# Attention and channel mix on one core: float32 product with v in the first eight heads, first head turned by TensorE

## The chip, the cores and the metric

The kernel runs on one core of one Trainium2 chip. The time is device time in microseconds (us) for one execution. A core has five engines that run side by side, each through its own list of instructions in order: TensorE (PE; its weight loads are shown apart, as PEld), VectorE (DVE), ScalarE (ACT), GpSimd (POOL) and SyncE (SP), which here issues all DMAs. [...]

## The reference

Batch 8, 8 heads, 1152 tokens, head size 64. Pairs of queries are averaged, so that each head has 576 queries and 1152 keys:

```
q_pool = q.reshape(B, H, S // 2, 2, D).mean(axis=3)
scores = (1 / sqrt(D)) * q_pool @ k^T
attn   = exp(scores - max);  attn = attn / (sum(attn) + 1e-9)
x      = attn @ v              # heads side by side: [8, 576, 512]
xk, xr = mu * x + (1 - mu) * (x shifted by one token)     # with mu_k, mu_r
kk     = relu(xk @ w_k);  vv = (kk * kk) @ w_v
out    = sigmoid(xr @ w_r) * vv
```

All is float32, with w_k 512 x 1024, w_v 1024 x 512 and w_r 512 x 512.

## The kernel before

TensorE takes float16 operands here, so every float32 operand is split into a high part (its float16 value) and a low part (the rest), and a product is made of two or three matmuls.

**Heads.** The 64 heads (n = 0 to 63, batch n // 8) come one after the other. `prep` (L421) loads a head's keys and values (`kr`, `vr`), splits the keys into high and low halves side by side in `kn` (L433 ScalarE, L438 VectorE for the first head, else GpSimd), turns `kn` by a transposing DMA into `ks1` (L441: upper 64 partitions the high, lower 64 the low halves) and copies the upper halves into `ks2` by another DMA (L444). It splits the scaled values into `vt` (high L449 ScalarE, low L452 VectorE) and makes `vb` (L455 GpSimd), a scaled float16 copy. `queries` (L387) does the like for a pair of heads: adds pairs of queries, splits, and turns by DMA (L416).

**Blocks.** A head has six blocks of 96 queries (`block`, L462). Scores of the nine key tiles go to PSUM (L482); VectorE takes the maximum over the tiles (L489); TensorE turns it (L492), VectorE ends the maximum (L495), TensorE spreads it (L497), ScalarE writes it as a row of the queries' low part (L500); the second scores (L506) add the low parts and take the maximum away. ScalarE's exponential (L512), shifted by 18, writes float32 weights to `pf`. The product then uses the upper 16 bits of each weight as a float16 number, read in place, and the lower 16 bits as an integer, which GpSimd scales to float16 in `pl` (L515; for the first 64 rows of a head into `pf` itself).

**Windows.** The product with v (`window`, L525) goes by five windows of up to 128 queries; the first holds 64 rows, its upper half and lower-bit half side by side ("side"). For each of nine key tiles there are two matmuls with the weights' upper bits (L541 with 65 columns, one of them the sum of the weights; L543 with 64), and one with the lower bits (L548). After the last window the side window's two halves are joined (L565, L567), and the rows are divided by their sums (L569 to L572). Every second head the result is turned into `xt`: in batch 0 by float32 transposes on TensorE (L597, L600), later by DMA.

**Weights.** w_k, w_r and w_v come in 20 tiles of 128 x 512 float32 (`weights`, L608) while the heads of batch 0 run. Each is split: absolute value on ScalarE (L630), the lowest bits from the top bytes of the low words on ScalarE (L633), two integer operations on VectorE (L635, L637), high part on ScalarE (L645), low part on GpSimd (L646).

**Feed-forward.** When all heads of a batch are done, tiles of 256 tokens go through `ff` (L693, matmuls at L709) between the heads of later batches.

**Order of work.** All of this is first noted as operations with an engine, a duration, the buffers read and written, and a due time (`op`, class `Issue`). A planner plays these durations through on a model of the engines, tries several orders, keeps the best by its own reckoning and writes the instructions of every engine in that order. The durations in the calls of `op` thus set the order, and changing one may change the order anywhere. To the planner DMA is one engine; `tail` is the time from its end to the landing.

The lines that the rest speaks of are in these functions.

Of the kernel before, what the change touches and what calls it, by code (L numbers as in the profile page):

```python
# [4 lines left out]

# [6 lines left out]
F32 = mybir.dt.float32  # L12
# [18 lines left out]
SQ = 0.25  # L31

# [3 lines left out]
LO, VLO = 2.0 ** -28, 2.0 ** -12  # L36
GUARD = 1e-9 * math.exp(SHIFT) * 2.0 ** -40
# [222 lines left out]
def kernel(  # L260
# [58 lines left out]
    nc.gpsimd.tensor_copy(identb, ident)  # L319
    negi = const.tile([P, P], F16, name="negi")  # L320
# [8 lines left out]
    qn = bufs("qn", 1, [P, 2, NQ, P], F16)  # L329
# [33 lines left out]
    def mus(n, m):  # L363
        t_ = const.tile([P, NG], F32, name=f"mu_{n}")
        o = const.tile([P, NG], F32, name=f"omu_{n}")
        mu[n] = (t_, o)
        op("DMA", 0.46, lambda: nc.sync.dma_start(t_, m.rearrange("(c p) -> p c", p=P)), w=[("mu", n)], key=60.0)
        sk = SK if n == "k" else 1.0
        op("DVE", 0.1, lambda: nc.vector.tensor_scalar(o, t_, -sk, sk, op0=ALU.mult, op1=ALU.add),
           r=[("mu", n)], w=[("omu", n)], key=62.0)  # L370
# [4 lines left out]
    nc.gpsimd.memset(qn[0][:, 1, :, D:P], 0.0)  # L375
    for t_ in ks2:
        nc.vector.memset(t_[D:P], 0.0)
        nc.vector.memset(t_[QN:QN + 1], SM)
    for t_ in vt:
        nc.vector.memset(t_[:, :, 2 * D:2 * D + 2], 1.0)  # L380
# [6 lines left out]
    def queries(n, key):  # L387

        b, h = divmod(n, H)
        i = n // 2 % 2  # L390
        qv = q[b, h:h + 2].rearrange("h (t f) d -> (h t) (f d)", f=2).rearrange("(j p) x -> p j x", p=P)
        JS = ((0, 5), (5, NQ))
        for j0, j1 in JS:
            js = slice(j0, j1)
            op("DMA", 0.36, lambda js=js: nc.sync.dma_start(qr[0][:, js], qv[:, js]), w=[("qr", j0)],
               key=key - 2 * NB * PER, tail=3.0)
            op("DVE", (j1 - j0) * D / 960 + 0.069, lambda js=js: nc.vector.tensor_tensor(
                qs[0][:, js], qr[0][:, js, 0:D], qr[0][:, js, D:2 * D], op=ALU.add),
               r=[("qr", j0)], w=[("qs", j0)], key=key, port=True)
            op("ACT", (j1 - j0) * P / 1200 + 0.093, lambda js=js, j1=j1, j0=j0: nc.scalar.activation(  # L400
                qn[0][:, 0, js].rearrange("p j (r d) -> p j r d", r=2),
                qs[0][:, js].unsqueeze(2).broadcast_to([P, j1 - j0, 2, D]), AF.Copy, scale=SQ),
               r=[("qs", j0)], w=[("qn", j0)], key=key + 1)
            op("DVE", (j1 - j0) * D / 960 + 0.069, lambda js=js: nc.vector.scalar_tensor_tensor(
                qn[0][:, 1, js, 0:D], qs[0][:, js], SQ, qn[0][:, 0, js, 0:D], op0=ALU.mult, op1=ALU.subtract),
               r=[("qs", j0), ("qn", j0)], w=[("qnl", j0)], key=key + 2, port=True)
            if n and j0 == 0:
                continue

            g0 = 0 if n else j0  # L410
            gs = slice(g0, j1)
            blocks = [(hh, jj, g) for g, g1 in JS for hh in (0, 1) for jj in range(NB)
                      if g0 <= g < j1 and hh * TQ + jj * QN < g1 * P and hh * TQ + (jj + 1) * QN > g * P]
            js_ = [g for g, _ in JS if g0 <= g < j1]
            for r_, m, t_ in ((0, "qn", "qT"), (1, "qnl", "qTl")):
                op("DMA", 1.25, lambda gs=gs, r_=r_: nc.sync.dma_start_transpose(  # L416
                    qT[i][:, r_, gs], qn[0][:, r_, gs].rearrange("p j x -> p (j x)")),
                   r=[(m, g) for g in js_] + ([("qn", g) for g in js_] if r_ else []),
                   w=[(t_, i) + b_ for b_ in blocks], key=key + 2, tail=2.0)

    def prep(n, key):  # L421
# [3 lines left out]
        def dma(o, src, buf):  # L425
# [3 lines left out]
        dma(vr[i], v[b, h].rearrange("(p c) d -> p c d", c=NC), ("vr", i))  # L429
        for c0, c1 in ((0, 5), (5, NC)):  # L430
# [10 lines left out]
        op("DMA", 1.3, lambda: nc.sync.dma_start_transpose(ks1[i], kn[i].rearrange("p c x -> p (c x)")),  # L441
           r=[(m, i, c0) for m in ("kn", "knl") for c0 in (0, 5)], w=[("ks1", i, 0), ("ks1", i, 5)],
           key=key + 1, tail=2.0)
        op("DMA", 0.47, lambda: nc.sync.dma_start(ks2[i][0:D], ks1[i][0:D]),  # L444
           r=[("ks1", i, 0), ("ks1", i, 5)], w=[("ks2", i)], key=key + 1, tail=2.5)
# [16 lines left out]
    def block(n, j, i, t):  # L462
# [49 lines left out]
        op("ACT", NC * QN / 1200 + 0.051, lambda: nc.scalar.activation(  # L512
            pf[:, :, HALF + rows.start:HALF + rows.stop], grid(0, NC), AF.Exp, bias=SHIFT, scale=0.125 / (2.0 * SQ)), r=[("s", z)], w=[("pf", j)], key=t + O_EXP)
# [11 lines left out]
    def window(n, w, t):  # L525
# [12 lines left out]

        def hi(c0, c1):
# [11 lines left out]
        for c0 in (0, 3, 6):  # L551
            op("PE", 3 * 0.0595, lambda c0=c0: hi(c0, c0 + 3),
               r=vk + [("pf", j) for j in js] + ([("pside",)] if side else []) + ([("a",)] if c0 or w else []),
               w=[("a",)], key=t)
        for c0, c1 in () if side else ((0, 5), (5, NC)):
# [9 lines left out]
        op("ACT", 0.34, lambda: nc.scalar.activation(cross[up], a_b[0:HALF, 0:VN], AF.Copy, scale=VLO),  # L565
           r=[("a",)], w=[("cross",)], key=t + O_EVAC)
        op("DVE", 0.36, lambda: nc.vector.tensor_tensor(a_b[up, 0:VN], a_b[up, 0:VN], cross[up], op=ALU.add),  # L567
           r=[("cross",), ("a",)], w=[("a",)], key=t + O_EVAC)
        op("DVE", 0.075, lambda: nc.vector.tensor_scalar(dz, u[:, :, D], GUARD, None, op0=ALU.add),  # L569
# [7 lines left out]
        if n >= H:  # L577
# [5 lines left out]
            for kx, x, to in (("xbh", xbh, xth), ("xbl", xbl, xtl)):  # L583
                op("DMA", 0.8, lambda x=x, to=to: nc.sync.dma_start_transpose(to.rearrange("p (k x) -> p k x", k=NW), x),
                   r=[(kx,)], w=[(kx, "t"), *old[1]], key=t + O_TURN, tail=2.0)
# [22 lines left out]
    def weights(n, w, kc, key, step):  # L608
        cols = w.shape[1]
        wv = w.bitcast(I32).rearrange("(c p) (f t) -> c p f t", p=P, t=2)  # L610
        for c in range(kc):
            for f in range(0, cols, 512):
# [9 lines left out]
                op("DMA", 0.36, lambda s3=s3, src=wv[c, :, f:f + 512]: nc.sync.dma_start(s3, src),  # L622
                   r=[("ks1", 1, 0), ("ks2", 0), ("vr", 1)] if iss.nw <= 2 else [], w=[ks, kl], key=key, tail=4.5)
# [8 lines left out]
                if True:  # L632
                    op("ACT", 0.57, lambda wl=wl, tops=tops: nc.scalar.activation(wl, tops, AF.Copy, bias=-0.49, scale=2.0 ** -5),  # L633
                       r=[ks, kl], w=[kl], key=key)
                    v_(0.6, lambda ui=ui, wl=wl: nc.vector.scalar_tensor_tensor(  # L635
                        ui, ui, 3, wl, op0=ALU.logical_shift_left, op1=ALU.bitwise_or), [kl, kf], [kf])
# [56 lines left out]
    def ff(t0, t1, key, tail):  # L693
# [49 lines left out]
        for s0 in range(0, n, P):  # L743
# [103 lines left out]
```

## Time and profile before

| | |
|---|---|
| median of 3 runs | 1133.76 us (1132.09 to 1134.21) |
| the profiled execution | 1131.52 us, its span 1129.7 us |
| busy: TensorE, VectorE, ScalarE, GpSimd | 1082.7, 867.5, 887.4, 818.7 us |
| mean granted TensorE clock | 0.992 of full speed |
| DMA | 135.81 MB, 120 GB/s on average |

A profile is one execution, and its span leaves out what lies around the first and the last instruction. In its rows, "x9" is a count, "128x96 f16<-128x864 f32" output and input as partitions x elements, and "<-" names what an engine waited for. Rows of one line give busy time and the mean in ns of one instruction; rows in order of time give start and duration in us. Matmuls overlap: each lasts some 0.2 us from entry to the last result, while the next enters after a small part of that, so the step from one start to the next tells their cost.

### The profile page before, as it was taken

What the parts mean: (1) busy time and instruction counts of PE and PEld (TensorE: products, weight loads), DVE (VectorE), ACT (ScalarE), POOL (GpSimd) and SP (SyncE); (2) the same over time, 40 slices, a digit from 0 to 9 for tenths busy, and PEclk for the clock granted to TensorE, in tenths of its full rate; (3) what the DMA queues carried; (4) which work ended last, traced back from release to release, by engine and by line L of the source; (5) the groups of instructions that cost most, each with busy time, mean ns of one, the idle gap of its engine ahead of it and who ended that gap; (6) DMA issues with size and microseconds to landing.
All of it is one profiled execution on the core that took longest, in us unless ns stands there. A gap on an engine that the chain in (4) does not pass through costs nothing.

```text
span 1129.7 us, 44739 instructions
## 1 busy us (share of the span) xinstructions
PE 1082.7 (96%) x18788; PEld 896.3 (79%) x18788; DVE 867.5 (77%) x1602; ACT 887.4 (79%) x1802; POOL 818.7 (72%) x940
## 2 busy tenths in 40 slices
PE   3878899999999999999999999999999999999998
PEld 3767787987888887978787888879797978887565
DVE  5899988888877887888778868788887888874320
ACT  4999997788888788887778787878888878875643
POOL 2777887887688777877778787778688877865431
PEclk9899999999999999999999999999999999999999
DMA  9998556665655665665665565666555555321000
GB/s 248 223 224 193 123 116 139 135 128 122 149 127 107 132 115 122 139 129 111 139 116 118 106 130 122 119 130 132 115 109 131 108 130 96 86 46 27 19 20 28
DMA packets 260011, 135.81 MB, mean 120 GB/s; under 512 B 195297, under 2 KB 232161, under 8 KB 259809
## 3 DMA queue, kind: packets, MB, share of 16 engines
q1 hardware_dynamic: 259808, 132.96, 56.2%
q8 instruction: 147, 2.41, 0.9%
q14 instruction: 56, 0.45, 0.1%
HBM read 67.11 MB, written 9.44 MB: 68 GB/s over the span
## 4 chain that ended last, share of the span: by engine, by line
PE 88%; DVE 4%; ACT 3%; issue 2%; DMA 1%; POOL 1%; SPq 0%; ACTq 0%; DVEq 0%; POOLq 0%
PE f L709 35%; PE s L482 12%; PE s L506 11%; PE a L541 7%; PE a L543 7%; PE a L548 6%; PE s L709 4%; PE s L492 2%; DVE mx L489 2%; PE a L709 2%; PE s L497 1%; ACT pf L512 1%; DMA mu_k<-in_moe_mu_k_dram 0%; DVE vt L452 0%; DVE mb L495 0%
## 5 line engine op out<-in xcount | busy, mean ns | idle before, releaser
L489 DVE TENSOR_REDUCE mx<-s 128x96 f16<-128x864 f32 x384 | 400.7, 1053 | 98.1 <-PE s L482 46.9
L515 POOL TENSOR_SCALAR pl<-pf 128x864 f16<-128x864 uint16 (+1 forms) x384 | 337.6, 879 | 119.0 <-ACT pf L512 86.0
L512 ACT ACTIVATE pf<-s 128x864 int32<-128x864 f32 x384 | 338.5, 891 | 80.1 <-PE s L506 58.0
L482 PE MATMUL s<-qT,ks 128*128 128x96 f16 x3456 | 216.8, 208 | 23.4 <-DMA ks<-kn 14.4
L543 PE MATMUL a<-vt,pf 128*128 128x64 f16 x2880 | 231.9, 193 | 0.5 <-issue 0.5
L541 PE MATMUL a<-vt,pf 128*128 128x65 f16 x2880 | 231.6, 193 | 0.7 <-DVE xb L572 0.4
L482 PEld LDWEIGHTS <-ks 128*128 128x128 f16 x3456 | 183.6, 99 | 48.7 <-DMA ks<-kn 14.4
L506 PE MATMUL s<-qT,ks 128*128 128x96 f16 x3456 | 213.6, 208 | 2.2 <-ACT qT L500 1.6
L541 PEld LDWEIGHTS <-pf 128*128 128x128 f16 x2880 | 199.7, 98 | 3.4
L506 PEld LDWEIGHTS <-ks 128*128 128x128 f16 x3456 | 179.2, 99 | 21.6 <-issue 3.1
L543 PEld LDWEIGHTS <-pf 128*128 128x128 f16 x2880 | 191.8, 98 | 5.4 <-issue 1.1
L495 DVE TENSOR_REDUCE mb<-s 96x1 f16<-96x128 f32 x384 | 109.1, 285 | 62.9 <-PE s L492 53.8
L500 ACT ACTIVATE qT<-s 1x96 f16<-1x96 f32 x384 | 92.5, 243 | 64.2 <-PE s L497 53.7
L709 PE MATMUL f<-xhk,wk_hi 128*128 128x256 f16 x496 | 135.1, 272 | 0.3 <-ACT r L736 0.3
L709 PE MATMUL f<-xlk,wk_hi 128*128 128x256 f16 x496 | 135.1, 272 | 0.0
L709 PE MATMUL f<-xhk,wk_lo 128*128 128x256 f16 x496 | 135.1, 272 | 0.0
L548 PE MATMUL a<-vb,pl 128*128 128x65 f16 x2304 | 124.1, 194 | 1.8 <-POOL pl L515 1.8
L709 PEld LDWEIGHTS <-wk_hi 128*128 128x128 f16 x1152 | 105.9, 98 | 10.4 <-issue 0.4
L548 PEld LDWEIGHTS <-pl 128*128 128x128 f16 x2304 | 99.9, 98 | 8.0 <-POOL pl L515 2.0
L740 POOL TENSOR_TENSOR gl<-g 128x512 f16<-128x512 f32 x72 | 79.2, 1101 | 35.4 <-ACT g L738 32.6
L438 POOL TENSOR_TENSOR kn<-kr,kn 128x320 f16<-128x320 f32 x126 | 96.4, 776 | 8.9 <-ACT kn L433 3.4
L492 PE MATMUL s<-identb,mx 128*96 128x128 f16 x384 | 87.2, 228 | 9.0 <-DVE mx L489 8.6
(104 smaller groups left out, 2152.9 us busy)
## 6 DMA issues: line engine op xcount, KB each, us to landing
kr<-in_k_dram SPq DMA_DIRECT2D x64, 288.0 KB, 3.2
vr<-in_v_dram SPq DMA_DIRECT2D x64, 288.0 KB, 3.3
qr<-in_q_dram SPq DMA_DIRECT2D x32, 320.0 KB, 3.5
ks<-ks SPq DMA_DIRECT2D x64, 144.0 KB, 3.0
out_dram<-em SPq DMA_DIRECT2D x36, 256.0 KB, 2.3
qr<-in_q_dram SPq DMA_DIRECT2D x32, 256.0 KB, 3.6
xt<-in_moe_w_k_dram SPq DMA_DIRECT2D x4, 512.0 KB, 6.4
st<-in_moe_w_k_dram SPq DMA_DIRECT2D x4, 512.0 KB, 5.6
```

Source lines behind the costliest of these rows:

```text
L438: lambda cs=cs, en=nc.vector if ve else nc.gpsimd: en.tensor_tensor(kn[i][:, cs, D:P], kr[i][:, cs], kn[i][:, cs, 0:D], op=ALU.subtract),
L482: nc.tensor.matmul(cols(c, c + 1), ks1[hp][:, c, :], qhi, start=(c == c0), stop=False, skip_group_check=True)
L489: op("DVE", 0.967, lambda: nc.vector.tensor_reduce(mxz, grid(0, NC).rearrange("p c q -> p q c"), axis=AX.X, op=ALU.max), r=[("s", z)], w=[ ...
L492: op("PE", 0.054, lambda: nc.tensor.matmul(s[0:QN, 0:P], mxz, identb, start=False, stop=False, skip_group_check=True), r=[("mx", z)], w=[( ...
L495: op("DVE", 0.199, lambda: nc.vector.tensor_reduce(mbz[0:QN], s[0:QN, 0:P], axis=AX.X, op=ALU.max), r=[("s", z)], w=[("mb", z)], key=t + O ...
L506: nc.tensor.matmul(cols(c, c + 1), ks2[hp][:, c, :], qlo, start=False, stop=True, skip_group_check=True)
L512: op("ACT", NC * QN / 1200 + 0.051, lambda: nc.scalar.activation(pf[:, :, HALF + rows.start:HALF + rows.stop], grid(0, NC), AF.Exp, bias=S ...
L515: op("POOL", NC * (r1 - r0) / 1000 + 0.066, lambda: nc.gpsimd.tensor_scalar(to, half(pf, U16, 0)[:, :, HALF + r0:HALF + r1], LO, 1.0, op0= ...
L541: nc.tensor.matmul(a_b[:, a0:a0 + VN], half(pf, F16, 1)[:, c, his], vt[jv][:, c, D:D + VN], start=(w == 0 and c == 0), stop=False, skip_gr ...
L543: nc.tensor.matmul(a_b[:, a0:a0 + D], half(pf, F16, 1)[:, c, his], vt[jv][:, c, 0:D], start=False, stop=(side and c == NC - 1), skip_group ...
L548: nc.tensor.matmul(a_b[:, a0:a0 + VN], pl[:, c, rows], vb[jv][:, c, 0:VN], start=False, stop=(c == NC - 1), skip_group_check=True)
L709: nc.tensor.matmul(ps, terms[i][0], terms[i][1], start=(first and i == 0), stop=(i == last), skip_group_check=True)
```

## The change

For the first eight heads (`N32 = 8`, batch 0) the product with v is made in float32: the exponential is not shifted and writes float32 weights that are used whole (`pw`, the same memory as `pf`); v is only scaled into float32 (`v32`, the memory of `vt`) by GpSimd; a window has one float32 matmul for each key tile; L515, L548, the joining of the side window and the splitting of v are left out for these heads.

The copy of the keys' upper halves into `ks2` goes from a DMA to GpSimd for these heads. The first head's keys and the high parts of its queries are turned by TensorE, into the score banks 0 and 1 as float16, and copied out by ScalarE and VectorE. The lowest bits of the model weights go from ScalarE (L633) to GpSimd. The loads of mu wait until the second head's `ks2` is written; the loads of the first four weight tiles, not of two, wait for the first heads' loads. A row of constants in `ks2` is written as float32 pairs, half as many elements. The planner's durations of DMAs are set anew, mostly higher (a head's load 0.36 to 0.98), and `prep(0)` is noted before `queries(0)`, the first load of v later.

```
+    N32 = 8
+    v32 = [t_.rearrange("p c x -> p (c x)").bitcast(F32).rearrange("p (c x) -> p c x", c=NC) for t_ in vt]
+    pw = pf.bitcast(F32)
...
-        op("DMA", 0.46, lambda: nc.sync.dma_start(t_, m.rearrange("(c p) -> p c", p=P)), w=[("mu", n)], key=60.0)
+        op("DMA", 0.46, lambda: nc.sync.dma_start(t_, m.rearrange("(c p) -> p c", p=P)), r=[("ks2", 1)], w=[("mu", n)], key=60.0)
...
-        nc.vector.memset(t_[QN:QN + 1], SM)
+        nc.vector.memset(t_[QN:QN + 1].bitcast(F32), SM2)
...
+                if n + r_ + j0 == 0:
+                    qt = s_b[1].bitcast(F16)[:, 0:j1 * P]
+                    op("PE", 0.33, lambda qt=qt, j1=j1: [nc.tensor.transpose(
+                        qt[:, j * P:(j + 1) * P], qn[0][:, 0, j], identb) for j in range(j1)],
+                       r=[("qn", 0)], w=[("s", 1)], key=key + 2)
+                    op("ACT", 0.59, lambda qt=qt, gs=gs: nc.scalar.copy(
+                        qT[0][:, 0, gs].rearrange("p j x -> p (j x)"), qt),
...
-            op("DMA", 0.36, lambda: nc.sync.dma_start(o, src), w=[buf], key=key - 2 * NB * PER, tail=2.8)
+            op("DMA", 0.98, lambda: nc.sync.dma_start(o, src), w=[buf], key=key - 2 * NB * PER + late, tail=2.2)
...
+        if n == 0:
+            kt = s_b[0].bitcast(F16)
+            op("PE", 0.6, lambda: [nc.tensor.transpose(kt[:, c * P:(c + 1) * P], kn[0][:, c], identb) for c in range(NC)],
+               r=[(m, 0, c0) for m in ("kn", "knl") for c0 in (0, 5)], w=[("s", 0)], key=key + 1)
...
+        if n < N32:
+            op("POOL", NC * P * 0.00105 + 0.07, lambda: nc.gpsimd.tensor_scalar(
+                ks2[i][0:D], ks1[i][0:D], 1.0, 1.0, op0=ALU.mult, op1=ALU.mult),
+               r=[("ks1", i, 0), ("ks1", i, 5)], w=[("ks2", i)], key=key + 1)
+        else:
+            op("DMA", 1.05, lambda: nc.sync.dma_start(ks2[i][0:D], ks1[i][0:D]),
...
+        if n < N32:
+            op("POOL", 0.67, lambda: nc.gpsimd.tensor_scalar(
+                v32[j][:, :, 0:D], vr[i], SV, 1.0, op0=ALU.mult, op1=ALU.mult),
+               r=[("vr", i)], w=[(x, j, c0) for x in ("vt", "vtl") for c0 in (0, 5)], key=key + 4)
+            return
...
+        p_, shift = (pw, 0.0) if n < N32 else (pf, SHIFT)
         op("ACT", NC * QN / 1200 + 0.051, lambda: nc.scalar.activation(
-            pf[:, :, HALF + rows.start:HALF + rows.stop], grid(0, NC), AF.Exp, bias=SHIFT, scale=0.125 / (2.0 * SQ)), r=[("s", z)], w=[("pf", j)], key=t + O_EXP)
+            p_[:, :, HALF + rows.start:HALF + rows.stop], grid(0, NC), AF.Exp, bias=shift, scale=0.125 / (2.0 * SQ)),
+           r=[("s", z)], w=[("pf", j)], key=t + O_EXP)
+        if n < N32:
+            return
...
+        def whole(c0, c1):
+            for c in range(c0, c1):
+                nc.tensor.matmul(a_b[:, a0:a0 + VN], pw[:, c, his], v32[jv][:, c, 0:VN],
+                                 start=(w == 0 and c == 0), stop=(c == NC - 1), skip_group_check=True)
...
-            op("PE", 3 * 0.0595, lambda c0=c0: hi(c0, c0 + 3),
+            op("PE", 3 * (0.115 if n < N32 else 0.0595), lambda c0=c0: (whole if n < N32 else hi)(c0, c0 + 3),
...
-                   r=[("ks1", 1, 0), ("ks2", 0), ("vr", 1)] if iss.nw <= 2 else [], w=[ks, kl], key=key, tail=4.5)
+                   r=[("ks1", 1, 0), ("ks2", 0), ("vr", 1)] if iss.nw <= len(stage) else [], w=[ks, kl], key=key, tail=3.1)
...
                 if True:
+                    op("POOL", 0.62, lambda wl=wl, tops=tops: nc.gpsimd.tensor_scalar(wl, tops, 2.0 ** -5, -0.49, op0=ALU.mult, op1=ALU.add),
+                       r=[ks, kl], w=[kl], key=key)
+                else:
                     op("ACT", 0.57, lambda wl=wl, tops=tops: nc.scalar.activation(wl, tops, AF.Copy, bias=-0.49, scale=2.0 ** -5),
...
-    queries(0, -20.0)
-    prep(0, -20.0)
+    prep(0, -24.0)
+    queries(0, -20.0)
     prep(1, -10.0)
```

More of the change, by code (lines that the diff above doesn't have):

```diff
@@ L4 @@
 import random
+import struct
 import concourse.bass as bass
@@ L394, in queries @@
             js = slice(j0, j1)
-            op("DMA", 0.36, lambda js=js: nc.sync.dma_start(qr[0][:, js], qv[:, js]), w=[("qr", j0)],
-               key=key - 2 * NB * PER, tail=3.0)
+            op("DMA", 0.2 * (j1 - j0), lambda js=js: nc.sync.dma_start(qr[0][:, js], qv[:, js]), w=[("qr", j0)],
+               key=key - 2 * NB * PER, tail=2.4)
             op("DVE", (j1 - j0) * D / 960 + 0.069, lambda js=js: nc.vector.tensor_tensor(
@@ L415, in queries @@
             for r_, m, t_ in ((0, "qn", "qT"), (1, "qnl", "qTl")):
-                op("DMA", 1.25, lambda gs=gs, r_=r_: nc.sync.dma_start_transpose(
+                if n + r_ + j0 == 0:
[5 more added lines that the diff above has]
+                        qT[0][:, 0, gs].rearrange("p j x -> p (j x)"), qt),
+                       r=[("s", 1)], w=[("qT", 0) + b_ for b_ in blocks], key=key + 2)
+                    continue
+                op("DMA", 0.248 * (j1 - g0), lambda gs=gs, r_=r_: nc.sync.dma_start_transpose(
                     qT[i][:, r_, gs], qn[0][:, r_, gs].rearrange("p j x -> p (j x)")),
                    r=[(m, g) for g in js_] + ([("qn", g) for g in js_] if r_ else []),
-                   w=[(t_, i) + b_ for b_ in blocks], key=key + 2, tail=2.0)
+                   w=[(t_, i) + b_ for b_ in blocks], key=key + 2, tail=1.3)
     def prep(n, key):
@@ L440, in prep @@
                r=[("kr", i), ("kn", i, c0)], w=[("knl", i, c0)], key=key + 1, port=True)
[L441 to L445, printed above, removed]
+        if n == 0:
+            kt = s_b[0].bitcast(F16)
+            op("PE", 0.6, lambda: [nc.tensor.transpose(kt[:, c * P:(c + 1) * P], kn[0][:, c], identb) for c in range(NC)],
+               r=[(m, 0, c0) for m in ("kn", "knl") for c0 in (0, 5)], w=[("s", 0)], key=key + 1)
+            kg = kt[:, 0:NC * P].rearrange("p (c x) -> p c x", c=NC)
+            op("ACT", 0.59, lambda: nc.scalar.copy(ks1[0][:, 0:5], kg[:, 0:5]), r=[("s", 0)], w=[("ks1", 0, 0)], key=key + 1)
+            op("DVE", 0.6, lambda: nc.vector.tensor_copy(ks1[0][:, 5:NC], kg[:, 5:NC]), r=[("s", 0)], w=[("ks1", 0, 5)], key=key + 1)
+        else:
+            op("DMA", 2.23, lambda: nc.sync.dma_start_transpose(ks1[i], kn[i].rearrange("p c x -> p (c x)")),
+               r=[(m, i, c0) for m in ("kn", "knl") for c0 in (0, 5)], w=[("ks1", i, 0), ("ks1", i, 5)],
+               key=key + 1, tail=1.1)
+        if n < N32:
[4 more added lines that the diff above has]
+            op("DMA", 1.05, lambda: nc.sync.dma_start(ks2[i][0:D], ks1[i][0:D]),
+               r=[("ks1", i, 0), ("ks1", i, 5)], w=[("ks2", i)], key=key + 1, tail=1.95)
+        if n < N32:
[3 more added lines that the diff above has]
+            return
+        if N32 <= n < N32 + NV:
+            op("POOL", 0.1, lambda: nc.gpsimd.memset(vt[j][:, :, 2 * D:2 * D + 2], 1.0), w=[("vt", j, 0), ("vt", j, 5)], key=key + 3)
         for c0, c1 in ((0, 5), (5, NC)):
@@ L551, in window @@
         for c0 in (0, 3, 6):
-            op("PE", 3 * 0.0595, lambda c0=c0: hi(c0, c0 + 3),
-               r=vk + [("pf", j) for j in js] + ([("pside",)] if side else []) + ([("a",)] if c0 or w else []),
+            op("PE", 3 * (0.115 if n < N32 else 0.0595), lambda c0=c0: (whole if n < N32 else hi)(c0, c0 + 3),
+               r=vk + [("pf", j) for j in js] + ([("pside",)] if side and n >= N32 else []) + ([("a",)] if c0 or w else []),
                w=[("a",)], key=t)
-        for c0, c1 in () if side else ((0, 5), (5, NC)):
+        for c0, c1 in () if side or n < N32 else ((0, 5), (5, NC)):
             op("PE", (c1 - c0) * 0.030, lambda c0=c0, c1=c1: lo(c0, c1),
@@ L564, in window @@
         up = slice(HALF, P)
[L565 to L569, printed above, removed]
+        if n >= N32:
+            op("ACT", 0.34, lambda: nc.scalar.activation(cross[up], a_b[0:HALF, 0:VN], AF.Copy, scale=VLO),
+               r=[("a",)], w=[("cross",)], key=t + O_EVAC)
+            op("DVE", 0.36, lambda: nc.vector.tensor_tensor(a_b[up, 0:VN], a_b[up, 0:VN], cross[up], op=ALU.add),
+               r=[("cross",), ("a",)], w=[("a",)], key=t + O_EVAC)
+        op("DVE", 0.075, lambda: nc.vector.tensor_scalar(dz, u[:, :, D], GUARD1 if n < N32 else GUARD, None, op0=ALU.add),
            r=[("a",)], w=[("den", z)], key=t + O_EVAC)
@@ L583, in window @@
             for kx, x, to in (("xbh", xbh, xth), ("xbl", xbl, xtl)):
[L584 to L585 removed]
+                op("DMA", 1.24, lambda x=x, to=to: nc.sync.dma_start_transpose(to.rearrange("p (k x) -> p k x", k=NW), x),
+                   r=[(kx,)], w=[(kx, "t"), *old[1]], key=t + O_TURN, tail=1.6)
             op("POOL", TQ * 0.0019 + 0.09, lambda: nc.gpsimd.tensor_tensor(
@@ L775, in ff @@
                r=[pk, ke], w=[km], key=key + O_DONE)
-            op("DMA", 0.36, lambda m_=m_, t=t0 + s0: nc.sync.dma_start(out_f[t:t + P], m_), r=[km], key=key)
+            op("DMA", 0.7, lambda m_=m_, t=t0 + s0: nc.sync.dma_start(out_f[t:t + P], m_), r=[km], key=key)
         return key
+    prep(0, -24.0)
     queries(0, -20.0)
-    prep(0, -20.0)
     prep(1, -10.0)
```

32 lines of the change are left out of this document (15 added, 17 removed).

## The prediction

> **What bounds the kernel now.** I read the page first: engine shares, then the slices.
>
> ```profile
> span 1129.7 us, 44739 instructions
> PE 1082.7 (96%) x18788; PEld 896.3 (79%) x18788; DVE 867.5 (77%) x1602; ACT 887.4 (79%) x1802; POOL 818.7 (72%) x940
> PE   3878899999999999999999999999999999999998
> ```
>
> TensorE is busy for 96% of the span, yet its first slices (28.2 us each) are 3, 8, 7, 8, 8. That is where the change acts: the eight heads of batch 0, and the weights, which are split at the same time. The busy times by stretch tell who sets the pace there. I cut at 14 us (first scores) and 137 us (first feed-forward matmul, the third row here).
>
> ```profile
> 14.00:137.00 123.00, 99.62 (x2034) 90.12 (x2035) 110.41 (x205) 108.00 (x212) 88.38 (x100) 0.93 0.88 202
> 137.00:1036.00 899.00, 893.26 (x16203) 751.73 (x16200) 727.58 (x1332) 729.63 (x1491) 696.02 (x793) 1.00 0.58 117
> L709 PEld LDWEIGHTS <-wk_hi x1152: 95/98/136, 137.3 to 1109.8; 128*128 128x128 f16 x192
> ```
>
> Columns of the stretches: PE, PEld, DVE, ACT, POOL busy, granted clock, DMA share, GB/s. From 137 us on PE is busy for 893.3 of 899 us: it is the bound, so work that starts a microsecond earlier ends one earlier. From 14 to 137 us it is not: VectorE is busy 110.4 of 123 us (90%), ScalarE 108.0 (88%), PE 99.6 by records that overlap. How much PE really has to do follows from spacings, first row to last:
>
> ```profile
> 119.32 0.55 PE L506 MATMUL s<-qT,ks 128*128 128x96 f16 x9
> 144.31 0.19 PE L541 MATMUL a<-vt,pf 128*128 128x65 f16 x1
> ...
> 145.37 0.19 PE L543 MATMUL a<-vt,pf 128*128 128x64 f16 x1
> ...
> L482 PE MATMUL s<-qT,ks 128*128 128x96 f16 x468 | 32.6, 222 | 22.4 <-DMA ks<-kn 14.4 <-ACT pf L512 7.3 <-issue 0.4
> L506 PE MATMUL s<-qT,ks 128*128 128x96 f16 x445 | 30.1, 220 | 1.6 <-ACT qT L500 1.3
> L543 PE MATMUL a<-vt,pf 128*128 128x64 f16 x360 | 30.0, 197 | 0.5 <-issue 0.5
> L541 PE MATMUL a<-vt,pf 128*128 128x65 f16 x360 | 30.0, 197 | 0.5 <-DVE xb L572 0.4
> L548 PE MATMUL a<-vb,pl 128*128 128x65 f16 x286 | 15.2, 195 | 1.8 <-POOL pl L515 1.8
> ```
>
> From 144.31 to 145.37 there are 36 matmuls, so 35 steps: 1.06/35 = 0.0303 us each. Nine score matmuls take 0.55 us, the last of which lasts about 0.21 (their mean is 220 ns): 0.34/8 = 0.0425 us. The last five rows count the stretch 14 to 137: (468+445) x 0.0425 = 38.8; (360+360+286) x 0.0303 = 30.5; the two small matmuls of each of some 50 blocks at the scores' pace, 4.3; 15 float32 transposes (below) 1.6. Sum 75.2 us, 61% of 123. So batch 0 is paced by VectorE and ScalarE, and PE has room.
>
> **The start.** Before 14.38 us PE has nothing.
>
> ```profile
> 5.34 0.83 DVE L438 TENSOR_TENSOR kn<-kr,kn 128x320 f16<-128x320 f32 x2
> 5.75 0.43 SPq L367 DMA_DIRECT2D mu_k<-in_moe_mu_k_dram  x1
> 10.94 1.31 SPq L441 DMA_TRANSPOSE ks<-kn  x1
> 14.38 2.34 PE L482 MATMUL s<-qT,ks 128*128 128x96 f16 x27 [14.38 <-DMA ks<-kn]
> ...
> 18.89 0.81 PE s L506 x9
> L400 ACT ACTIVATE qn<-qs 128x640 f16<-128x640 f32 x4 | 2.9, 735 | 1.3 <-DVE qs L397 1.3
> DVE omu_k L369 <- DMA mu_k<-in_moe_mu_k_dram: 5.3, 1, 5.3
> ```
>
> The first head's keys are split at 5.34+0.83 = 6.17 us, but the transposing DMA leaves SP at 10.94, just as mu_k lands (issued 5.75), and lands at 14.38. VectorE too sits 5.3 us behind its small operation on mu_k, with the queries' low halves queued after it. The change removes both waits: mu is loaded once ks2 of the second head is written, and the first head's keys and the high parts of five query blocks (640 queries, all 576 of that head among them) are turned by PE. Nine f16 transposes into an idle PE at 0.11 us each (no row for f16; the float32 ones below take 0.105) are 1.0, about 0.25 each way to hand over, and a copy of 640 columns, 0.74 by L400's 735 ns: 6.17+1.0+0.5+0.74 = 8.4 us. The queries' chain is as long and shares ScalarE; I take 9.9 us, a gain of 4.5, between 6 (8.4) and 0 (the next loads come late instead). Late next is the queries' low half, still a DMA: ready near 7, landing near 10.4 if it takes the 3.4 of the keys' one (10.94 to 14.38); the second scores of block 0 come 4.5 us after the first (14.38 to 18.89), so it is covered. POOL's copy of the keys into ks2, some 1.25 us (below), is done near 10 as well. Two waits are added on SP. The mu loads wait for POOL's second key copy, with later loads queued behind; VectorE's small operations on mu come late in the plan (nobody needs mu before the first feed-forward): 0, with today's 5.3 as the bound if they are placed too early. The first four weight tiles, not two, wait for the first heads' loads: 0, as the weights are needed only at the end of batch 0.
>
> **VectorE and ScalarE in batch 0.** These forms go, in the stretch 14 to 137:
>
> ```profile
> L452 DVE SCALAR_TENSOR_TENSOR vt<-vr,vt 128x320 f16<-128x320 f32 x7 | 4.7, 677 | 0.1
> L452 DVE SCALAR_TENSOR_TENSOR vt<-vr,vt 128x256 f16<-128x256 f32 x8 | 4.4, 548 | 0.0
> L567 DVE TENSOR_TENSOR a<-a,cross 64x65 f32<-64x65 f32 x7 | 1.7, 244 | 0.3
> L633 ACT ACTIVATE st<-st 128x512 int32<-128x512 uint8 x9 | 6.2, 686 | 0.1
> L633 ACT ACTIVATE xt<-xt 128x512 int32<-128x512 uint8 x9 | 6.1, 681 | 0.1
> L449 ACT ACTIVATE vt<-vr 128x320 f16<-128x320 f32 x7 | 3.3, 468 | 2.3 <-DMA vr<-in_v_dram 2.0 <-PE a L541 0.3
> L449 ACT ACTIVATE vt<-vr 128x256 f16<-128x256 f32 x7 | 2.9, 416 | 0.1
> L565 ACT ACTIVATE cross<-a 64x65 f32<-64x65 f32 x7 | 1.5, 218 | 0.4 <-PE s L497 0.3
> ```
>
> VectorE: 4.7+4.4+1.7 = 10.8, less 1.2 for head 8, whose v is still split: -9.6, to 100.8. ScalarE: 12.3+6.2+1.5 = 20.0, less 0.9 for head 8: -19.1, to 88.9. At the present filling of VectorE (110.4/123 = 0.898) its 100.8 us take 112.2: -10.8 us.
>
> **POOL.** It loses the low bits of the weights of attention, and gains two kinds of copies.
>
> ```profile
> L515 POOL TENSOR_SCALAR pl<-pf 128x864 f16<-128x864 uint16 x40 | 37.8, 945 | 13.9 <-ACT pf L512 9.9 <-DVE f L635 1.2 <-DVE mb L495 0.8
> L515 POOL TENSOR_SCALAR pf<-pf 128x576 f16<-128x576 uint16 x9 | 8.0, 894 | 12.0 <-ACT pf L512 11.6
> L515 POOL TENSOR_SCALAR pl<-pf 128x288 f16<-128x288 uint16 x8 | 3.5, 433 | 0.6
> L455 POOL TENSOR_SCALAR vb<-vr 128x576 f16<-128x576 f32 x8 | 5.4, 673 | 4.8 <-DMA vr<-in_v_dram 3.9 <-PE s L492 0.4
> ```
>
> Of L515's 49.3 us about 3.6 belong to head 8: -45.7. The vb scaling becomes the float32 v scaling, same shape: 0. Added: 20 weight tiles of 512 at 673/576 ns an element, 0.60 each, 12.0; 8 key copies of 1152 elements, 1.25 by L515's 945/864 per element (the DMA it replaces frees SP's queue of 8 issues): 10.0. Net 88.4-45.7+22.0 = 64.7 of some 112 us: not a bound. The key copy, in order on POOL, can sit behind a v scaling that waits for its load, as one did here for 3.9 us, and the second scores wait for it: 0 to 3.9 us, once, while the transfers are full; I take 0.5. The weight's low bits sit in a chain of five steps over tiles loaded far ahead: 0, with the weights' half-empty POOL as cover.
>
> **The float32 product.** A window's 27 f16 matmuls (18 in the side window) become 9 in float32 with 65 columns. No float32 product stands in the trace; the nearest rows are the transposes of float32.
>
> ```profile
> L597 PEld LDWEIGHTS a<-ident,xb x20: 138/144/231, 56.5 to 141.8; 128*128 128x128 f32 x20
> L597 PE MATMUL a<-ident,xb x20: 272/295/476, 56.5 to 141.9; 128*128 128x128 f32 x20
> 141.77 0.40 PE L597 MATMUL a<-ident,xb 128*128 128x128 f32 x2
> L541 PEld LDWEIGHTS <-pf 128*128 128x128 f16 x2880 | 199.7, 98 | 3.4
> ```
>
> Two take 0.40, the last 0.295: 0.105 us apart, for 128 columns. Bounds for one product of 65 columns: 65/128 of that, 0.053, if it costs as a transpose does; four such steps with a full reload, 0.42, if the two halves of each operand meet in separate passes whose weight load (144 ns beside 98 in f16) sets the pace. Between them: four passes at the f16 pace, 4 x 0.0303 = 0.121. I take 0.121, nearer to the lower row, as loads hide behind matmuls in every f16 row. 360 x 0.121 = 43.6 in place of 30.5: PE +13.1, to 88.3 us, 79% of 112. It is hidden as long as VectorE is later; but three engines then stand at 79 to 90%, and a tighter PE delays the reduces: +2.3 us (bounds 0 and 6, half of PE's added work).
>
> [...]
>
> **What else moves.** The planner's DMA prices rise (0.36 to 0.98 for a head's load, 1.3 to 2.23 for a key transpose), so the whole order changes. After 137 us PE idles 5.7 us in 899, so no order gains more there; as much may be lost: 0, bounds -3 and +3.
>
> **Sum.** -4.5 (start) -10.8 (VectorE) +0.5 (key copy) +2.3 (PE) = -12.5 us. The profiled execution took 1131.52 us (span 1129.7), so about 1119; the runs' median is 1133.76, so 1121.3, said as **1121 us**.
>
> **Rivals.**
> 1. Forecast: VectorE stays the pacer of batch 0, shorter. 1111 (first scores at 8.4, and VectorE filled to 95%, half way from 90% to the 99% of PE after 137: -6 -16.9) to 1129 (start gains nothing, PE penalty 6). Chance 0.66.
> 2. Transfers pace batch 0. For: a DMA share of 0.88 in it against 0.58 after, and POOL's 3.9 us for v. Against: eight key copies and two transposes leave the queues, and PE's longest idle there after the start, 7.3 us ahead of L482, was ended by ScalarE. Then the start's 4.5 and little else: 1129 to 1133. Chance 0.13.
> 3. PE becomes the bound, by the price of one float32 product. PE's other work is 75.2-30.5 = 44.7; batch 0 may last 127.5 us without loss (123 plus the earlier start); at 95% filling this leaves (121.1-44.7)/360 = 0.21 us each. That is the point from which it decides. At 0.21: no change, 1134 (chance 0.07). At 0.42: (44.7+151.2)/0.95 = 206, +79 us, 1213 (chance 0.14 for anything clearly above 0.21). For: the float32 load is 46 ns longer than in f16, and two transposes stand 0.105 apart where f16 columns would give 128 x 0.0303/65 = 0.06. Against: two f16 passes of 128 columns would be 0.12, so passes alone explain 0.105.
>
> [...]
>
> **How the numbers follow.** About 0.2% (2.3 us) is what a measurement of this kernel tells from no change. Faster: rival 1 and most of 2, 0.79. Same: the rest of 2 and the 0.21 case, 0.07. Slower: 0.14. The range 1110 (rival 1's low end, one lower for the order) to 1133 holds 1 and 2; the dear product stays outside.
>
> **What would show it.** First scores near 10 us and feed-forward matmuls from about 124 instead of 137; VectorE near 101 us in between, ScalarE near 89, POOL near 65. Nine float32 products in 1.0 to 1.2 us: right; in 2 us or more: rival 3, and PE's slices read 9 in batch 0. First scores early but the feed-forward not: rival 2, with waits on loads. Wrong altogether if PE after 137 us idles by more than 3 us over today's.

## The result and the profile after

The changed kernel is slower: 1172.85 us, median of 4 runs (1160.36 to 1174.59), against 1133.47 (1132.09 to 1134.21, four runs) before, a ratio of 1.033 (95% interval 1.029 to 1.037). The prediction was 1121 us, between 1110 and 1133. The profiled execution is the quickest of the four, 1160.36 us with a span of 1158.6, 28.9 more than before; the other three, at 1172.7 to 1174.6, left no trace. Here and below, where the runs of a kernel spread, the ratio is taken from those within 1.5% of its quickest; this leaves out, among others, one run of 2513.57 us (no head in float32, below) and one of 1834.88 (the kernel before).

The page of the changed kernel, the lines that answer those of before:

```profile
span 1158.6 us, 44098 instructions
PE 1132.6 (98%) x18514; PEld 951.5 (82%) x18514; DVE 859.2 (74%) x1579; ACT 869.8 (75%) x1760; POOL 788.7 (68%) x916
PE   6999999999999999999999999999999999999998
```

The slices of batch 0, once 3, 8, 7, 8, 8, now read 6, 9, 9, 9, 9. The stretches, cut at the same points of the work (columns as before: PE, PEld, DVE, ACT, POOL busy, clock, DMA share, GB/s), and the first feed-forward matmul:

```profile
14.00:162.00 148.00, 140.31 (x1621) 135.10 (x1620) 95.96 (x176) 89.02 (x171) 62.30 (x76) 1.00 0.64 158
...
162.00:1061.00 899.00, 892.61 (x16198) 753.86 (x16197) 730.97 (x1332) 728.91 (x1485) 688.32 (x788) 1.00 0.56 117
...
L753 PEld LDWEIGHTS <-wk_hi x1152: 95/98/135, 162.3 to 1138.8; 128*128 128x128 f16 x192
```

Batch 0 ends at 162.3 instead of 137.3 us: 25.0 of the 28.9 us. From there to the end it is 996.3 us instead of 992.4. VectorE and ScalarE did shed what was forecast (96 and 89 us), but over 148 us that is 65% and 60%: they wait now, and TensorE is the bound. The waits of 14 to 160 us say the same, ScalarE and VectorE waiting for TensorE (us in total, times, longest):

```profile
ACT qT L536 <- PE s L533: 33.3, 26, 6.2
...
DVE mb L531 <- PE s L528: 21.0, 21, 3.6
ACT pf L549 <- PE s L542: 20.7, 21, 2.7
DVE mx L525 <- PE s L518: 18.9, 19, 2.7
```

What TensorE does there is in its rows in order of time. L582 is the float32 product, L518 the first scores:

```profile
8.66 2.32 PE L518 MATMUL s<-qT,ks 128*128 128x96 f16 x27 [1.55 <-ACT qT L428]
...
38.60 1.51 PE L582 MATMUL a<-vt,pf 128*128 128x65 f32 x6
...
40.73 4.04 PE L582 MATMUL a<-vt,pf 128*128 128x65 f32 x18
...
44.76 0.92 PE L518 MATMUL s<-qT,ks 128*128 128x96 f16 x9
...
47.52 0.54 PE L518 MATMUL s<-qT,ks 128*128 128x96 f16 x9 [0.36 <-ACT pf L549]
...
51.08 2.17 PE L582 MATMUL a<-vt,pf 128*128 128x65 f32 x18
```

Two things are to be seen. The scores start at 8.66 us, as meant. And a product is dear twice over. Its records (720 of them, so two for each of the 360 products), the last of which lasts 0.275 us, stand (2.17 - 0.275)/17 = 0.1115 us apart from 48 us on: 0.223 us for a product, where the forecast had 0.121. Up to 47 us the same work on TensorE takes nearly twice as long again: nine score matmuls 0.92 instead of 0.54, 18 records 4.04 instead of 2.17 (0.213 us apart, not 0.112). That is the half pace spoken of below. The clock column of this profile reads 1.00 throughout, so the nine scores are the better gauge here; in the trace of the product alone (below) the same half pace stands beside a clock of 0.50.

The loads of the weights in front of these records, and the records themselves:

```profile
L582 PEld LDWEIGHTS a<-vt,pf x720: 186/192/338, 15.6 to 168.0; 128*128 128x128 f32 x180
L582 PE MATMUL a<-vt,pf x720: 275/275/442, 15.7 to 168.0; 128*128 128x65 f32 x180
```

### The profile page after: what moved, and what is told of

The parts are those of the page before. It is cut to its first block, busy times and chain, and to the rows that moved or that the text cites. A ratio compares the mean times of both kernels' runs of the same rounds, so it can differ in the third digit from the quotient of the medians.

```text
span 1158.6 us, 44098 instructions
## 1 busy us (share of the span) xinstructions
PE 1132.6 (98%) x18514; PEld 951.5 (82%) x18514; DVE 859.2 (74%) x1579; ACT 869.8 (75%) x1760; POOL 788.7 (68%) x916
## 4 chain that ended last, share of the span: by engine, by line
PE 92%; DVE 4%; ACT 2%; issue 1%; DMA 0%; SPq 0%; DVEq 0%; ACTq 0%
PE f L753 33%; PE s L518 12%; PE s L542 12%; PE a L582 8%; PE a L587 6%; PE a L589 6%; PE a L594 5%; PE s L753 4%; PE s L528 2%; DVE mx L525 2%; PE a L753 2%; PE s L533 1%; ACT pf L549 1%; DVE xb L619 0%; DMA kr<-in_k_dram 0%
## 5 line engine op out<-in xcount | busy, mean ns | idle before, releaser
L549 ACT ACTIVATE pf<-s 128x864 int32<-128x864 f32 (+1 forms) x384 | 338.4, 890 | 108.2 <-PE s L542 81.0
L556 POOL TENSOR_SCALAR pl<-pf 128x288 f16<-128x288 uint16 x336 | 299.2, 890 | 134.1 <-ACT pf L549 113.2
L518 PE MATMUL s<-qT,ks 128*128 128x96 f16 x3456 | 215.7, 208 | 4.0 <-ACT pf L549 2.5
L518 PEld LDWEIGHTS <-ks 128*128 128x128 f16 x3456 | 184.4, 99 | 26.5 <-issue 5.1
L587 PE MATMUL a<-vt,pf 128*128 128x65 f16 x2520 | 202.2, 193 | 1.5 <-DVE xb L619 1.4
L589 PE MATMUL a<-vt,pf 128*128 128x64 f16 x2520 | 202.4, 193 | 0.0
L587 PEld LDWEIGHTS <-pf 128*128 128x128 f16 x2520 | 174.2, 98 | 4.3 <-issue 0.5
L589 PEld LDWEIGHTS <-pf 128*128 128x128 f16 x2520 | 166.9, 97 | 7.7 <-issue 2.2
L594 PE MATMUL a<-vb,pl 128*128 128x65 f16 x2016 | 107.4, 193 | 0.0
L582 PE MATMUL a<-vt,pf 128*128 128x65 f32 x720 | 101.7, 294 | 1.0 <-DVE xb L619 0.9
L784 POOL TENSOR_TENSOR gl<-g 128x512 f16<-128x512 f32 x72 | 78.5, 1092 | 32.4 <-ACT g L782 28.9
L582 PEld LDWEIGHTS a<-vt,pf 128*128 128x128 f32 x720 | 95.6, 209 | 1.7 <-issue 1.0
```

Of the source, the lines that this page charges most:

```text
L518: nc.tensor.matmul(cols(c, c + 1), ks1[hp][:, c, :], qhi, start=(c == c0), stop=False, skip_group_check=True)
L556: op("POOL", NC * (r1 - r0) / 1000 + 0.066, lambda: nc.gpsimd.tensor_scalar(to, half(pf, U16, 0)[:, :, HALF + r0:HALF + r1], LO, 1.0, op0= ...
L582: nc.tensor.matmul(a_b[:, a0:a0 + VN], pw[:, c, his], v32[jv][:, c, 0:VN], start=(w == 0 and c == 0), stop=(c == NC - 1), skip_group_check ...
L587: nc.tensor.matmul(a_b[:, a0:a0 + VN], half(pf, F16, 1)[:, c, his], vt[jv][:, c, D:D + VN], start=(w == 0 and c == 0), stop=False, skip_gr ...
L589: nc.tensor.matmul(a_b[:, a0:a0 + D], half(pf, F16, 1)[:, c, his], vt[jv][:, c, 0:D], start=False, stop=(side and c == NC - 1), skip_group ...
L594: nc.tensor.matmul(a_b[:, a0:a0 + VN], pl[:, c, rows], vb[jv][:, c, 0:VN], start=False, stop=(c == NC - 1), skip_group_check=True)
```

## The experiments

Theory at the start: the float32 product costs 0.223 us and makes TensorE the bound, and the half pace adds to that. Rivals: the plan, made for a product of half the price; and the other parts of the change. Each kernel was timed against the kernel before on the same chip.

**The change without its product** (N32 = 0; the copies of the keys' upper halves kept for eight heads by a switch of their own):

```
-    N32 = 8
+    N32, NK = 0, 8
...
-        if n < N32:
+        if n < NK:
```

> The change without its float32 product: the product with v is float16 in all heads, as before; the start, the key copies and the weights' low bits on GpSimd and the new DMA prices stay. Theory (the float32 product alone is the loss: 720 records 0.1115 us apart make a product 0.223 us, not 0.121, and TensorE ran at half pace until 47 us): first scores near 8.7 us, first feed-forward matmul at 124 to 132, time 1118 to 1130. Rival (the other parts lose: the plan, the key copies behind waits on GpSimd): 1140 or more.

Measured: 1136.52 us, ratio 1.0034 (1.0021 to 1.0047). So the product is the loss: without it 36 of the 39 us are gone. But the theory's 1118 to 1130 was missed: the rest of the change gains nothing. A suspect is seen in its batch 0: GpSimd, which keeps the attention weights' low bits here and has two more jobs, is as full as VectorE (110.45 and 110.67 us of 124.6). The start alone, below, tests it.

```profile
14.00:138.60 124.60, 99.29 (x1980) 88.13 (x1981) 110.67 (x202) 97.55 (x198) 110.45 (x127) 0.92 0.79 190
```

**The product alone**, put into the kernel before:

```
+        if n < N32:
+            op("POOL", 0.67, lambda: nc.gpsimd.tensor_scalar(
+                v32[j][:, :, 0:D], vr[i], SV, 1.0, op0=ALU.mult, op1=ALU.mult),
...
+            op("PE", 3 * (0.115 if n < N32 else 0.0595), lambda c0=c0: (whole if n < N32 else hi)(c0, c0 + 3),
```

> The kernel before with nothing changed but the float32 product in heads 0 to 7 (float32 weights, v scaled by GpSimd, no low bits). Theory: first scores at 14.4 as before, first feed-forward matmul at 162 to 175 instead of 137, time 1160 to 1178. Rival (the product is hidden and the rest of the change loses): 1125 to 1140.

Measured: 1167.89 us, ratio 1.0313 (1.0296 to 1.0330), first feed-forward matmul at 163.2. As the theory has it; the product alone makes nearly the whole loss.

**The true price in the plan:**

```
-            op("PE", 3 * (0.115 if n < N32 else 0.0595), lambda c0=c0: (whole if n < N32 else hi)(c0, c0 + 3),
+            op("PE", 3 * (0.223 if n < N32 else 0.0595), lambda c0=c0: (whole if n < N32 else hi)(c0, c0 + 3),
```

> The change with the planner's price of a float32 product set from 0.115 to the measured 0.223 us; the work is the same. Theory (TensorE paces batch 0 with work that no order takes away): within 8 us of the change, 1150 to 1173. Rival (the order was planned for a product of half the cost, and this is what loses): 1140 or less.

Measured: 1169.31 us (1155.19 to 1172.89), ratio 1.0284 (1.0219 to 1.0350). The order is not the main cause. The spread of 18 us with one and the same program pointed to the pace, and the trace, of the run of 1172.89 us, bears it out: nine scores take 0.88 to 0.93 us up to 70 us, where the change's profiled run had its full pace from 48 us on.

**A warm start:** 14 float16 matmuls whose result nobody reads, in TensorE's idle time before 14 us: five at the start, three more behind the queries' turns, two behind L528 of each of the blocks 0, 1 and 2.

```
+    def idle(m):
+        for _ in range(m):
+            nc.tensor.matmul(f_b[:, 0:512].rearrange("p (a b) -> p a b", a=4), identb,
+                             identb.unsqueeze(1).broadcast_to([P, 4, P]), start=True, stop=True, skip_group_check=True)
+
+    idle(5)
...
```

> The change with 14 float16 matmuls of 512 columns more, their result unused, in TensorE's idle time before 14 us (5 ahead of the first turns, 3 after them, 2 after each of the first three blocks' turned maxima); order otherwise the same. Theory (half pace because the clock is not granted while too little TensorE work has gone by, and it holds once granted, float32 products or not): nine scores take 0.55 us from 14 us on instead of 0.92, first feed-forward matmul near 146, time 1140 to 1148. Rival (float32 products themselves run at half pace or take the clock away again): nine scores at 0.9 us after 16 us again, time 1158 to 1176.

Measured: 1146.23 us (1145.40 to 1146.59), ratio 1.0121 (1.0106 to 1.0136). Its rows on TensorE:

```profile
14.28 0.54 PE L525 MATMUL s<-qT,ks 128*128 128x96 f16 x9 [0.44 <-ACT pf L556]
14.65 0.85 PE L589 MATMUL a<-vt,pf 128*128 128x65 f32 x6
...
L760 PEld LDWEIGHTS <-wk_hi x1152: 95/98/135, 148.2 to 1123.8; 128*128 128x128 f16 x192
```

Nine scores take 0.54 us from 14 us on, six product records 0.85 instead of 1.51, and batch 0 ends at 148.2 us. Against the profiled execution of the change that is 14.1 us earlier, against its median 26.6 us less: by this comparison the half pace cost an estimated 14 to 27 us of the 39; that it lasted longer in the three runs without a trace than in the one with is likely, not shown. With the float32 product the full pace comes later: with the same start and the product in float16 nine scores take 0.54 to 0.55 us from 19.66 us on (to 31.90 at least), with float32 only from 47.52 on.

The full pace held in these four runs with products of 65 columns: nine scores take 0.54 or 0.55 us in the trace up to 63 us, 20 us hold 233 to 248 matmuls from 40 to 140 us, and the runs lie within 1.2 us of one another with a mean granted clock of 1.00 in each. This refutes the rival for this kernel. The product alone did not hold it: in the trace of the product alone nine scores take 0.55 us at 26.83 us, TensorE then waits 3.73 us, and from 32.73 to 55.37 us they take 0.88 to 0.92 again. Here the clock column does read 0.50, from 40 to 60 us: the same half pace stands beside 1.00 in one trace and beside 0.50 in the other.

**Half the columns:** eight of nine products of a window stream only the right 33 columns of v (the left half of v is left out), on top of the warm start; one run, then four more.

```
+                x0 = 32 if c else 0
+                nc.tensor.matmul(a_b[:, a0 + x0:a0 + VN], pw[:, c, his], v32[jv][:, c, x0:VN],
```

> The warm start again, but eight of the nine float32 products of a window stream 33 columns of v instead of 65 (the left half of v is left out there, so the result is not the reference's). Two records make one product. Passes set the price: records of 33 columns stand about 0.057 to 0.07 us apart instead of 0.1115, first feed-forward matmul 25 to 30 us earlier than in the warm start. Weight loads set the price (two slow loads to a record): 0.105 to 0.112 as before, first feed-forward matmul within 4 us of 148.

> The half-column kernel (eight of nine float32 products stream 33 columns, left half of v left out there), timed in several runs. Theory (the clock follows how much the array streams, and a product that waits for its weight loads streams little; with half the columns still less): mean granted clock under 0.985 and over 1160 us in most runs, where the warm start with 65 columns had 1.0 and 1146 in all. Rival (the one look fell by chance on a bad run): clock 1.0 and 1141 to 1148 in most runs.

The product's rows in the first run (a merged row names the shape of its first record), with nine scores in front of them:

```profile
52.90 0.55 PE L549 MATMUL s<-qT,ks 128*128 128x96 f16 x9
...
53.34 2.15 PE L590 MATMUL a<-vt,pf 128*128 128x65 f32 x18
...
L590 PEld LDWEIGHTS a<-vt,pf x720: 186/192/338, 14.6 to 176.3; 128*128 128x128 f32 x180
L590 PE MATMUL a<-vt,pf x720: 248/277/455, 14.7 to 176.4; 128*128 128x33 f32 x160, 128*128 128x65 f32 x20
```

The stretch from 40 to 100 us of the warm start (columns as before):

```profile
40.00:100.00 60.00, 57.12 (x733) 54.98 (x731) 42.83 (x80) 40.36 (x78) 29.30 (x34) 1.00 0.75 191
```

The same stretch of the half columns, in one of the four later runs:

```profile
40.00:100.00 60.00, 58.45 (x518) 57.61 (x517) 31.40 (x58) 28.45 (x53) 20.09 (x23) 0.64 0.51 141
```

Eighteen records, mostly of 33 columns, take 2.15 us where those of 65 take 2.17, and the nine scores show that the pace was full. So the columns do not set the price here. What stands with every record regardless is one weight load of 128 x 128 in float32 (720 loads, 720 records; the expectation spoke of two to a record). The trace before has one more width: two of its float32 transposes (L597), of 128 columns, start 0.11 us apart (56.65 and 56.76 us). With 33, 65 and 128 columns the step is 0.11 us. That the load sets it is my estimate from these three steps: no run changed the load alone, and its rows differ, 192 ns in the products and 144 in the transposes (medians).

The rest of the first expectation failed, and told more than it asked: half the streaming should have changed nothing, yet the kernel took 1168.77 us, and 1179.86 (1166.78 to 1185.49) in the four later runs, ratio 1.038 (1.033 to 1.043), 22 to 34 us more than the warm start. The second expectation held in its figures: the granted clock was lower again, 0.958 to 0.976 on average in all five runs, and 0.64 between 40 and 100 us in the second trace, with PE busy 58.45 of 60 us by its records, after 1.00 from 14 to 40 us. So a busy row went with a lost clock here: in the same order of the same instructions, with 33 columns in place of 65, it was lost in five runs of five, and with 65 (1.00 in each) in none of four. That the clock follows what the array streams is the theory's; these runs do not show why it fell.

**The start alone:** float16 product, key copies of heads 1 to 7 by DMA, low bits on ScalarE, as before; the start and the DMA prices of the change. The second line switched off is the one that puts the low bits on GpSimd.

```
-    N32 = 8
+    N32, NK = 0, 1
...
-                if True:
+                if False:
```

> Of the change only the start and the DMA prices: float16 product in all heads, the key copies of heads 1 to 7 by DMA again, the weights' low bits on ScalarE again. Theory (the change without the float32 product lost because GpSimd kept the attention weights' low bits and got two new jobs: busy 110.5 of 124.6 us): GpSimd back near 88 us in batch 0, first scores near 8 us, first feed-forward matmul at 131 to 135, time 1126 to 1131. Rival (the early start gives nothing, as VectorE and ScalarE are filled later all the same): 1131.5 to 1135.

Measured: 1135.05 us, ratio 1.0026 (1.0017 to 1.0035). The theory falls. GpSimd is back at 93.9 of 123 us, and most of the loss stays. Scores start 5.8 us earlier and the kernel is ahead at 100 us (40 blocks reduced, against 35) and still at 200 (77 against 76, and 184 feed-forward matmuls against 160), but from 200 to 1100 us TensorE idles 9.1 us instead of 4.0, by the busy times of its stretches of 100 us.

**The DMA prices** were the suspect: alone in the kernel before, taken out of the start alone, and taken out of the warm start with the true price. The edits are the durations and `tail` values of the DMA lines of the diff.

> The kernel before with nothing but the new DMA prices (durations and landing times) in the plan: the same instructions in another order. Theory (the order that these prices give costs about what the early start gains): 1135 to 1141. Rival (the prices are harmless; something in the start itself gives the gain back): 1130 to 1134.

> The start alone (first head's keys and five query blocks turned by TensorE, mu and the weight tiles later, its key copy on GpSimd) with the old DMA prices; product float16 in all heads. Theory: first scores near 8 us carry through a stretch that TensorE then bounds, 1126 to 1130. Rival (batch 0 is not held by its start): 1131 to 1136.

> The warm start with all eight heads in float32, the true product price and the old DMA prices. Theory (DMA prices cost 3 to 8 us of order, whatever the product): 1133 to 1138. Rival (they cost nothing here, where TensorE is full in batch 0): 1139 to 1143.

Measured: 1131.82 us alone, ratio 0.9990 (0.9981 to 0.9999); 1140.31 for the start with the old prices, 1.0073 (1.0059 to 1.0088), its first scores only at 12.8; 1160.34 (1153.51 to 1166.63) for the warm start, 1.0246 (1.0206 to 1.0285). All three against my theory, and the last two above the range of the rival as well: alone the prices cost nothing, and the start does better with them. The warm start with the old prices says less, as its clock was lower: its runs of 1153.51, 1159.97, 1160.71 and 1166.63 us had a mean granted clock of 0.997, 0.990, 0.989 and 0.982, where the same kernel with the new prices had 0.999 to 1.0 (next). How much of its loss is order and how much pace stays open. Which part of the start makes the later order worse stays open; it was not tried.

**The warm start with the true price:**

> The warm start with the planner's price of a float32 product set from 0.115 to 0.223 us. Theory (TensorE is full in batch 0, its order is worth little): within 3 us of the warm start, 1143 to 1149. Rival (the wrong price cost several us by order): 1135 to 1142.

Measured: 1140.91 us (1140.81 to 1141.31), ratio 1.0078 (1.0065 to 1.0091): 5.3 us better than with the wrong price. With the pace settled, the price in the plan is worth that much; the rival held.

**Fewer heads in float32,** with the warm start and the true price: four (key copies on GpSimd), two and none (key copies by DMA from head 1 on: `N32, NK = 2, 1` and `0, 1`), and two without the idle matmuls.

```
-    N32 = 8
+    N32, NK = 4, 8
```

> The warm start with the float32 product in heads 0 to 3 only, float16 in 4 to 7, and the true price 0.223 in the plan; key copies and low bits of the weights on GpSimd in all of batch 0. Theory: TensorE has 75 + 4 x 6.2 = 100 us of work, VectorE about 103, GpSimd about 87, none over 90% of 120 us; first feed-forward matmul at 124 to 131, time 1119 to 1128, better than both kernels. Rival (the heads in float32 are paced by TensorE and the float16 ones by VectorE and GpSimd, so the halves do not share their slack): 1131 to 1140.

> The warm start with the float32 product in heads 0 and 1 only and its true price, the key copies of heads 1 to 7 by DMA, the weights' low bits on GpSimd. By the rows so far no engine is full in batch 0: TensorE 75 + 2 x 6.2 = 87 us, VectorE about 108, ScalarE about 94, GpSimd about 90. Theory (the float32 product loses only where TensorE becomes the bound, and two heads are not enough for that; relief of ScalarE and GpSimd and the early start count): 1124 to 1130, better than both kernels. Rival (VectorE holds batch 0, and what is ahead there is lost again in the order of the stretch that TensorE bounds, as in the start alone): 1131 to 1137.

> The version with two heads in float32, with none: warm start, weights' low bits on GpSimd, key copies by DMA, product float16 in all heads. Theory (two heads in float32 relieve GpSimd of about 11 us and TensorE can carry them): slower than with two heads, 1130 to 1135. Rival (the gain of that version comes from the start and the clock alone, the float32 product gives nothing in any dose): 1125 to 1129.

> The version with two heads in float32, without the 14 idle matmuls. Theory (they open the clock before the float32 products; without them these run at half pace until float16 work prevails): 6 x 2 windows of products at double cost, 8 to 16 us slower than with them, 1135 to 1145. Rival (VectorE holds the first heads anyway, the clock costs nothing): 1127 to 1131.

Four heads: 1140.17 us, ratio 1.0061 (1.0031 to 1.0091), in three groups that go by the mean granted clock: 1133.2 to 1134.9 at 0.995 to 0.998, 1145.4 to 1146.3 at 0.985 to 0.986, 1161.8 and 1161.9 at 0.968. Even the best group is no better than the kernel before, 1131.83 beside it. The trace is of a run of the last group, and shows a clock of 0.50 with products of 65 columns:

```profile
49.90 0.54 PE L549 MATMUL s<-qT,ks 128*128 128x96 f16 x9
...
54.14 0.92 PE L549 MATMUL s<-qT,ks 128*128 128x96 f16 x9
...
60.00:110.00 50.00, 48.96 (x346) 48.82 (x344) 22.86 (x40) 20.39 (x40) 20.54 (x27) 0.50 0.38 105
```

Between the first two rows TensorE waited twice, 0.4 and 0.6 us. Nine scores took 0.55 us again at 116.53 us, after the last float32 product (109 us).

Two heads: **1128.57 us** (1128.02 to 1129.72), ratio 0.9961 (0.9948 to 0.9975), the one version that beats both kernels. None: 1131.21, ratio 0.9984 (0.9972 to 0.9995). Two heads cold: 1140.14, from 1129.90 to 1156.25. Four of these twelve runs are within 4 us of the warm median and two some 27 us above it, so the idle matmuls buy the steadiness more than the best time; the mean clock reads 0.992 to 0.997 in all of them and tells them apart no better than in the change. Batch 0 cut at 129 us, first with two heads:

```profile
14.00:129.00 115.00, 99.76 (x1887) 91.87 (x1887) 102.81 (x191) 96.49 (x191) 87.87 (x105) 0.97 0.85 203
```

The same stretch with none:

```profile
14.00:129.00 115.00, 90.19 (x1835) 81.37 (x1834) 103.68 (x194) 94.35 (x189) 97.47 (x116) 0.90 0.83 209
```

With two, GpSimd has 9.6 us less and TensorE is fuller, with the clock at 0.97 instead of 0.90. The intervals of the two just overlap, so that the product itself gains in this dose is likely, not shown.

## Why the prediction was wrong, point by point

- **The start** was right as a row and wrong as a gain: first scores at 8.66 us, between the 8.4 and the 9.9 of the text. Its 0.25 us for a hand-over was an estimate without a row: in the trace after, VectorE's copy starts 0.19 us after the keys' transposes end (6.03 and 6.22 us), the scores 0.05 after ScalarE's copy (8.61 and 8.66). But the start alone costs 0.26%, so the sum's -4.5 us was not earned; that it would carry through a stretch bounded by TensorE failed, since the order of that stretch let 5 us of idle time in. "0, bounds -3 and +3" for what else moves was too narrow.
- **VectorE, ScalarE and GpSimd** were right: 100.8, 88.9 and 64.7 us were forecast, 96.0, 89.0 and 62.3 measured. What failed is that VectorE stays the pacer, and with it the -10.8 us.
- **The float32 product** is the step that broke the sum: 0.121 us taken, 0.223 measured, 360 x 0.102 = 36.7 us more TensorE work than forecast. I took the lower row because loads hide behind matmuls in float16 (98 ns a load, a matmul every 0.0303 us); here the records stand 0.11 us apart with 33 columns as with 65, and a product has two. The forecast held half of it: its 0.105 us for a float32 transpose was close to that step, but I scaled it by the columns to get the low bound of 0.053. The rival had the right place, its decision point of 0.21 us and the load as the likely reason, with a chance of 0.21 for both of its cases, and both of its signs came: nine products in 2.17 us, slices of 9 in batch 0. At full pace its formula gives (44.7 + 80.3)/0.95 - 127.5 = +4 us for 0.223; the warm start with the true price measured +9 over the 1131.83 of the kernel before beside it.
- **The clock** is the step that was missing. TensorE was taken to run at full pace; with the change it ran at half pace to 47 us in the profiled execution, 14 us of the 28.9. The trace before held the hint: the stretch read 0.93, and nine scores took 0.88 to 0.93 us up to 24 us and again from 29.7 to 33.5.
- **The chances** count the whole of rival 2 as faster (0.66 + 0.13 = 0.79), where the text gives it most of it.
- **The four passes** of the 0.121 were an estimate that no run shows, nor the 0.121 itself: a product left two records, 0.223 us in all, and 18 records took 2.15 us with mostly 33 columns against 2.17 with 65. The load's 144 ns beside 98, which the prediction had in its own rows, got too little weight.

## What to carry to other kernels

Price a matmul in another type by what its records are measured to cost, and count the records: 33, 65 and 128 columns in float32 all took 0.11 us a record here, and a product took two. An engine with 39% of room is not free for work that is cheap only by a row of another type; work out the price at which it becomes the bound (0.21 us here) before the price that one likes. And look at a fixed group of matmuls as a gauge of pace (nine scores, 0.54 or 0.92 us): in the warm start the mean clock was 1.00 with products of 65 columns and 0.958 to 0.976 with 33, and its 14 matmuls in idle time ahead of them brought the nine scores to 0.54 us at 14 us instead of 47. What decides when the clock is lost with 65 columns stays open.

## What the runs showed of the hardware

- A float32 product of 128 x 128 by 128 x 65 left two records, 0.1115 us apart, and 33 columns cost the same (18 records in 2.15 us against 2.17).
- TensorE's pace was halved for 33 us in the change's profiled execution (nine scores 0.92 us, not 0.54) while its records were nearly back to back (31.96 of 33 us busy). The clock column did not show it: it read 1.00 there, and to 70 us in the run with the true price. It read 0.50 where a full pace had been lost again (product alone, 40 to 60 us; four heads, 60 to 110 us).
- The same program took 1133, 1146 or 1162 us (four heads) with a mean granted clock of 0.997, 0.985 or 0.968; two heads without the idle matmuls took 1130 to 1156 us at 0.992 to 0.997.
